# Where the output projection puts its four token tiles between two doubles of the score loop

## The chip, the cores and the metric

The kernel runs on one core of one Trainium2 chip. The metric is the device time of one execution in microseconds (us); of several runs the median is given.

## The reference

Four layers over 2048 tokens of width 448: attention, feed-forward, and both once more with the same weights. All is float32. The attention has 16 query heads of 28 columns and a single head of keys and values.

```
def _A_ref(x, wq, wk, wv, wo):
    q = (x @ wq).reshape(B, S, H, Dh) -> B, H, S, Dh
    k = x @ wk
    v = x @ wv
    scores = jnp.einsum("bhqd,bkd->bhqk", q, k) * (Dh ** -0.5)
    p = _softmax(scores, axis=-1)
    o = jnp.einsum("bhqk,bkd->bhqd", p, v)
    return o -> B, S, H * Dh @ wo

x = A_x
x = x + _A_ref(_layernorm(x, axis=-1), A_wq, A_wk, A_wv, A_wo)
x = x + _B_ref(_layernorm(x, axis=-1), B_w_gate, B_w_up, B_w_down)
x = x + _A_ref(_layernorm(x, axis=-1), A_wq, A_wk, A_wv, A_wo)
x = x + _B_ref(_layernorm(x, axis=-1), B_w_gate, B_w_up, B_w_down)
```

The change concerns the last matmul of the attention, `o @ wo`, and the addition of its result to x.

## The kernel before

**Stages.** For each of the two attention layers the kernel projects queries, keys and values, then runs the score loop (`scores`, line 565), then the feed-forward. Tokens are held in four chunks of 512, each of four token tiles of 128 rows; `xres` holds x in these tiles. The order of instructions on each engine is the order in which the program writes them.

**The score loop.** A group (c, g) is one chunk of 512 queries and four heads; there are 16 groups in a layer. A group has 16 steps, one for each 128 keys (kt). A step n (line 595) issues 12 score matmuls, three passes (z) over four heads (j): the contraction has 32 rows, and the four heads lie in the four 32-row parts of TensorE. Heads 0 to 2 go to the three banks of a triple, `threes[n % 2]`, head 3 goes to a single bank. ACT then takes the exponentials: in an even step the single bank first (L616), then the triple (L617); in an odd step the triple (L611), and, from a copy `raw` that DVE has made of the single bank (L613), head 3 (L614).

Two steps, 2d and 2d + 1, make a double d. After its odd step come `pv(d - 1)` (line 640), the product of the previous double's exponentials with the values, into a single bank that DVE then adds to an accumulator (L657), and `between(d)` (line 620).

**PSUM.** Of eight banks, six are the two triples, and two are single banks:

```
single = lambda d: banks[6 + d % 2]
three, one = threes[n % 2], single(n // 2 + n)   # step n
free, one = threes[0], single(d + 1)                # between(d)
po = single(d + 1)                                  # pv(d)
```

So in double d the even step's head 3 goes to `single(d)`, the odd step's to `single(d + 1)`, and pv(d - 1) to `single(d)`, after the even step's exponential has read it. When `between(d)` runs, the even step's triple `threes[0]`, the odd step's single bank and the bank of pv(d - 1) hold nothing that later work needs, once their readers are done. The next double's even step writes `threes[0]` and `single(d + 1)`, its odd step writes `threes[1]` and `single(d)`.

**The output projection.** When all four groups of a chunk are normalised, the chunk is put on `todo`, and `between` takes it from there at kt equal 10. This happens for chunks 0, 1 and 2, so three times in a layer; chunk 3 is projected after the loop by other lines. `outproj(c, t, po)` (line 582) issues 12 matmuls for one token tile t, four groups by three products of high and low parts, into bank `po`, and returns a function that issues the add of `po` to `xres` on DVE (L591). In the kernel before, tiles 1, 2 and 3 go to the three banks of `threes[0]`; their three adds are issued after all 36 matmuls; then tile 0 goes to the odd step's single bank, with its add behind it.

The function `forward` is called a second time under a condition on the softmax's sums (`full` is true there); that second pass is not run with these inputs.

Of the kernel before, what the change touches and what calls it, by code (L numbers as in the profile page):

```python
# [52 lines left out]
def forward(  # L53
# [278 lines left out]
    class Attention:  # L332
# [232 lines left out]
        def scores(self, ff):  # L565
            next(switch)
            with tc.tile_pool(name=f"at{self.layer}", bufs=1, reuse_waits="tile") as wp:
# [4 lines left out]
                single = lambda d: banks[6 + d % 2]  # L572
# [9 lines left out]
                def outproj(c, t, po, gs=range(NG)):  # L582
                    oh, ol = on[c]
                    ts_ = slice(P * t, P * t + P)
                    for g in gs:
                        for z, (a, b) in enumerate(((oh, woh), (oh, wol), (ol, woh))):
                            nc.tensor.matmul(
                                po[:, 0:D], a[:, g, ts_], b[:, g, :], start=(g + z == 0), stop=(g == NG - 1 and z == 2)
                            )
                    if gs[-1] == NG - 1:  # L590
                        return lambda: nc.vector.tensor_tensor(  # L591
                            xres[:, 4 * c + t, :], po[:, 0:D], xres[:, 4 * c + t, :], ALU.add
                        )
# [26 lines left out]
                def between(d):  # L620

                    i, kt = divmod(2 * d, NT)
                    free, one = threes[0], single(d + 1)
                    if full:
                        self.lent = free[:, 0, :]
                        if 6 <= kt < 14:
                            self.advance(min(NM // 4, NM * (i + 2) - self.done))
                        if kt == 14 and i + 1 < len(GR):
                            self.places[i + 1](free[:, 1, :])
                    if not todo or kt != 10:  # L630
                        return
                    c = todo.pop()
                    adds = []
                    for t in (1, 2, 3):
                        adds.append(outproj(c, t, free[:, t - 1, :]))
                    for f in adds:
                        f()
                    outproj(c, 0, one)()

                def pv(d):  # L640

# [66 lines left out]
                for n in range(last):  # L708
                    i, kt = divmod(n, NT)
                    if kt == 0 and i + 1 < len(GR):  # L710
                        self.parts(i + 1)
                    if kt == 3 and i + 1 < len(GR) and not full:
                        self.rows(i + 1)
                    if kt == 12 and i + 2 < len(GR):
                        self.stack(i + 2)
                    if i in (2, 3) and kt == 8:
                        load_wo(i - 2)
                    if n == NT and ff.nxt:
                        ff.nxt.below(nc.sync)
                    if kt == 8 and 10 < i <= 11 + FG:  # L720
                        ff.W[i - 11] = weights(i - 11)
                    step(n)
                    if not full and n == 1:
                        self.maxima(NC - 1, (6,))
                    if n in later:
                        later.pop(n)()
                    d, odd = divmod(n, 2)
                    if odd:
                        if d:
                            pv(d - 1)  # L730
                        between(d)
                        if d in due:
                            due.pop(d)()
# [322 lines left out]
```

## Time and profile before

| | us |
|---|---|
| median of 3 runs | 1984.74 |
| lowest and highest run | 1983.31, 1984.76 |
| the profiled execution, its time | 1984.76 |
| the profiled execution, its span | 1983.0 |
| exponentials of the score loop, layer 0 | 65.3 to 570.9 |
| exponentials of the score loop, layer 1 | 1047.1 to 1552.5 |
| output projection, L587, inside the loops | 6 times |
| granted TensorE clock | 1.00 |

How to read it: the span runs from the first to the last instruction; the time has a little around it. Engines are PE (TensorE matmul), PEld (its weight loads, which overlap the matmuls), DVE, ACT, POOL and SP. A row of the timeline has the start in us, the length in us, the engine, the line of the kernel, the operation and the tiles as out<-in; in brackets stands how long the engine was idle before it and what ended that. Several like instructions that follow each other are merged, with their count. In names, numbers of buffers are left out: `three` is either triple, `bank` any single bank. A row of the waits has the total, how often, and the longest. The lines themselves stand in the prediction.

### The profile page before, as it was taken

What the parts mean: (1) busy time and instruction counts of PE and PEld (TensorE: products, weight loads), DVE (VectorE), ACT (ScalarE), POOL (GpSimd) and SP (SyncE); (2) the same over time, 40 slices, a digit from 0 to 9 for tenths busy, and PEclk for the clock granted to TensorE, in tenths of its full rate; (3) what the DMA queues carried; (4) which work ended last, traced back from release to release, by engine and by line L of the source; (5) the groups of instructions that cost most, each with busy time, mean ns of one, the idle gap of its engine ahead of it and who ended that gap; (6) DMA issues with size and microseconds to landing.
All of it is one profiled execution on the core that took longest, in us unless ns stands there. A gap on an engine that the chain in (4) does not pass through costs nothing. (4 is left out here: it accounts for less than half of the span.)

```text
span 1983.0 us, 44658 instructions
## 1 busy us (share of the span) xinstructions
PE 1968.8 (99%) x18507; PEld 1323.7 (67%) x18507; DVE 814.1 (41%) x1413; ACT 1277.6 (64%) x2137; POOL 526.5 (27%) x570
## 2 busy tenths in 40 slices
PE   9999999999999999999999999999999999999998
PEld 7544545445458999999984444454454699988887
DVE  7444543544434222322554335435454432222323
ACT  4899797997953333333349998979979533333332
POOL 4212111132213233332341221111222133233320
PEclk9999999999999999999999999999999999999999
DMA  5101020121210011100131111102111100011102
GB/s 163 55 21 31 24 51 22 31 58 28 72 33 6 27 32 32 32 21 22 51 107 35 30 31 30 44 12 59 32 52 48 33 17 25 23 32 32 32 1 76
DMA packets 93382, 77.52 MB, mean 39 GB/s; under 512 B 23510, under 2 KB 76374, under 8 KB 93174
## 3 DMA queue, kind: packets, MB, share of 16 engines
q1 hardware_dynamic: 92886, 74.16, 13.5%
q8 instruction: 146, 2.39, 0.5%
q14 instruction: 62, 0.51, 0.1%
q10 hardware_dynamic: 288, 0.46, 0.1%
HBM read 55.06 MB, written 18.74 MB: 37 GB/s over the span
## 5 line engine op out<-in xcount | busy, mean ns | idle before, releaser
L647 PE MATMUL bank<-pt,vsb 128*32 128x512 f32 x4096 | 493.3, 598 | 0.5
L604 PE MATMUL bank<-qstack,keys 32*128 32x512 f32 x1536 | 484.1, 424 | 1.7 <-DVE xres L591 1.7
L604 PE MATMUL three<-qstack,keys 32*128 32x512 f32 x4608 | 461.4, 425 | 1.5 <-DVE vt L538 1.2
L604 PEld LDWEIGHTS three<-qstack,keys 32*128 32x128 f32 x4608 | 254.1, 182 | 295.3 <-ACT pt L617 181.1
L321 PE MATMUL bank<-xh,wgh 64*128 64x512 f32 x1728 | 437.7, 389 | 0.1
L611 ACT ACTIVATE pt<-three 128x1536 f32<-128x1536 f32 x256 | 372.3, 1454 | 0.6 <-ACT pt L617 0.3
L617 ACT ACTIVATE pt<-three 128x1536 f32<-128x1536 f32 x256 | 372.1, 1453 | 0.0
L321 PE MATMUL bank<-xh,wgl 64*128 64x512 f32 x1404 | 363.1, 390 | 0.0
L321 PE MATMUL bank<-xl,wgh 64*128 64x512 f32 x1296 | 328.5, 389 | 0.0
L321 PE MATMUL bank<-wdh,h 64*128 64x448 f32 x1776 | 327.0, 363 | 0.3 <-ACT h L892 0.2
L891 DVE TENSOR_TENSOR sg<-bank,sg 128x512 f32<-128x512 f32 x111 | 76.7, 691 | 493.4 <-ACT sg L890 484.3
L647 PEld LDWEIGHTS bank<-pt,vsb 128*32 128x32 f32 x4096 | 107.1, 109 | 250.2 <-issue 152.6
L613 DVE COPY raw<-bank 128x512 f32<-128x512 f32 x256 | 177.3, 693 | 230.6 <-PE bank L604 227.7
L321 PEld LDWEIGHTS bank<-xh,wgh 64*128 64x128 f32 x1728 | 256.8, 184 | 16.1 <-issue 0.9
L798 POOL TENSOR_TENSOR xres<-stage,xres 128x448 f32<-128x448 f32 x107 | 126.7, 1206 | 490.2 <-ACT stage L797 490.2
L657 DVE TENSOR_TENSOR o<-bank,o 128x512 f32<-128x512 f32 x224 | 154.8, 691 | 240.9 <-PE bank L647 236.3
L321 PEld LDWEIGHTS bank<-wdh,h 64*128 64x128 f32 x1776 | 238.6, 184 | 12.9 <-issue 2.0
L604 PEld LDWEIGHTS bank<-qstack,keys 32*128 32x128 f32 x1536 | 243.7, 183 | 4.5 <-DVE xres L591 3.6
L328 ACT COPY seen<-bank 128x1 f32<-128x1 f32 x660 | 80.5, 163 | 237.0 <-PE bank L321 234.6
L321 PEld LDWEIGHTS bank<-xh,wgl 64*128 64x128 f32 x1404 | 212.1, 184 | 13.3
L321 PE MATMUL bank<-wdl,h 64*128 64x448 f32 x888 | 213.7, 367 | 0.0
L890 ACT ACTIVATE sg<-bank 128x512 f32<-128x512 f32 x111 | 66.7, 601 | 221.2 <-PE bank L321 212.2
(136 smaller groups left out, 2265.8 us busy)
## 6 DMA issues: line engine op xcount, KB each, us to landing
o<-rd SPq DMA_DIRECT2D x32, 256.0 KB
qraw<-qd SPq DMA_DIRECT2D x128, 56.0 KB
qd<-stage SPq DMA_DIRECT2D x30, 224.0 KB
xt<-xn SPq DMA_DIRECT2D x28, 224.0 KB
wdr<-in_B_w_down_dram SPq DMA_DIRECT2D x28, 224.0 KB
xn<-xt SPq DMA_DIRECT2D x7, 768.0 KB
wr<-in_B_w_gate_dram SPq DMA_DIRECT2D x28, 192.0 KB
wr<-in_B_w_up_dram SPq DMA_DIRECT2D x28, 192.0 KB
```

The source lines that it names most:

```text
L321: nc.tensor.matmul(po, a, b, start=start, stop=stop, skip_group_check=True)
L328: nc.scalar.copy(seen[:, i : i + 1], po[:, 0:1])
L604: nc.tensor.matmul(three[:, j, :] if j < 3 else one, k[js, kp, ks], q[js, part, :], start=(z == 0), stop=(z == 2), tile_position=(32 * j, 0),)
L611: nc.scalar.activation(pt, three, AF.Exp, scale=SCALE)
L613: nc.vector.tensor_copy(raw, one)
L617: nc.scalar.activation(pt, three, AF.Exp, scale=SCALE)
L647: nc.tensor.matmul(po[32 * j : 32 * j + 32, :], vsb[:, n % NT, :], pts[n][j], start=(n == 2 * d), stop=(n > 2 * d), skip_group_check=True,)
L657: nc.vector.tensor_tensor(acc, in_turn(po), acc, ALU.add)
L798: nc.gpsimd.tensor_tensor(r, s, r, ALU.add)
L890: nc.scalar.activation(by_tile(sg), in_turn(pg[0]), AF.Silu)
L891: nc.vector.tensor_tensor(by_tile(sg), in_turn(pg[1]), by_tile(sg), ALU.mult)
```

## The change

In `between`, the four token tiles are put elsewhere and in another order. Tiles 0 and 1 go to the first two banks of `threes[0]`, and their two adds are issued after these 24 matmuls. Then tile 2 goes to the odd step's single bank `single(d + 1)`, with its add behind it. Then tile 3 goes to `single(d)`, the bank of pv(d - 1), which the next double's odd step writes; its add comes last. `outproj` and all else is as before.

```
-                    adds = []
-                    for t in (1, 2, 3):
-                        adds.append(outproj(c, t, free[:, t - 1, :]))
-                    for f in adds:
+                    for f in [outproj(c, t, free[:, t, :]) for t in range(2)]:
                         f()
-                    outproj(c, 0, one)()
+                    outproj(c, 2, one)()
+                    outproj(c, 3, single(d))()
```

## The prediction

> **What bounds the kernel now.** I read the page first, then the waits, then the two attention stages as stretches, then the timeline around one output projection.
>
> ```profile
> span 1983.0 us, 44658 instructions
> PE 1968.8 (99%) x18507; PEld 1323.7 (67%) x18507; DVE 814.1 (41%) x1413; ACT 1277.6 (64%) x2137; POOL 526.5 (27%) x570
> ```
>
> PE looks full, but that is an average over stages, and as matmuls are pipelined and their ends modelled, a busy PE is not PE at its peak. The change touches only the score loop, so that stage decides. The two loops as stretches (span, then busy time and instructions of PE, PEld, DVE, ACT, POOL):
>
> ```profile
> 65.30:575.00 509.70, 507.92 (x5269) 228.97 (x5270) 230.96 (x414) 475.26 (x514) 109.17 (x111) 1.00 0.14 36
> 1048.00:1560.00 512.00, 510.77 (x5284) 231.43 (x5277) 230.76 (x414) 474.87 (x514) 108.41 (x108) 1.00 0.14 35
> ```
>
> ACT is busy for 475.3 of 509.7 us. The rest must be few, large holes, and the waits say which (total, times, longest):
>
> ```profile
> ACT pt L616 <- PE bank L604: 63.6, 8, 10.7
> ...
> PEld bank L604 <- DVE xres L591: 3.6, 6, 0.6
> ```
>
> Nearly all the time that ACT waits for scores lies in 8 places, the longest 10.7 us. Here is one, in ACT's timeline (start, length, idle before it in brackets):
>
> ```profile
> 203.82 1.46 ACT L611 ACTIVATE pt<-three 128x1536 f32<-128x1536 f32 x1
> 205.17 0.62 ACT L614 ACTIVATE pt<-raw 128x512 f32<-128x512 f32 x1
> 216.26 0.60 ACT L616 ACTIVATE pt<-bank 128x512 f32<-128x512 f32 x1 [10.47 <-PE bank L604]
> 216.76 1.45 ACT L617 ACTIVATE pt<-three 128x1536 f32<-128x1536 f32 x1
> 218.09 1.46 ACT L611 ACTIVATE pt<-three 128x1536 f32<-128x1536 f32 x1
> 219.44 0.62 ACT L614 ACTIVATE pt<-raw 128x512 f32<-128x512 f32 x1
> 219.96 0.59 ACT L616 ACTIVATE pt<-bank 128x512 f32<-128x512 f32 x1
> ```
>
> Away from the hole the four exponentials of a double run back to back: from one L616 to the next is 219.96 - 216.26 = 3.70 us, with no idle. So ACT sets the pace of the score loop, and the only time to be had from this change is the hole of 10.47 us, in which PE does the output projection of one chunk. It occurs three times in a layer (line 630: the doubles with kt equal 10 in the group after a finished chunk), six times in all. The last one looks the same as the first, both at the add and at ACT:
>
> ```profile
> 1454.62 0.62 DVE L591 TENSOR_TENSOR xres<-bank,xres 128x448 f32<-128x448 f32 x1 [0.67 <-PE bank L587]
> ```
>
> ```profile
> 1456.34 0.60 ACT L616 ACTIVATE pt<-bank 128x512 f32<-128x512 f32 x1 [10.45 <-PE bank L604]
> ```
>
> **Inside the hole.** The timeline of PE and its neighbours:
>
> ```profile
> 202.81 0.69 DVE L613 COPY raw<-bank 128x512 f32<-128x512 f32 x1 [1.12 <-PE bank L604]
> ...
> 204.50 0.47 PE L587 MATMUL three<-woh,onh 128*128 128x448 f32 x1
> ...
> 204.69 0.69 DVE L657 TENSOR_TENSOR o<-bank,o 128x512 f32<-128x512 f32 x1 [1.19 <-PE bank L647]
> ...
> 209.26 0.37 PE L587 MATMUL three<-woh,onl 128*128 128x448 f32 x1
> 209.47 0.36 PE L587 MATMUL three<-woh,onh 128*128 128x448 f32 x1
> ...
> 211.70 0.36 PE L587 MATMUL three<-woh,onl 128*128 128x448 f32 x1
> 211.90 0.36 PE L587 MATMUL bank<-woh,onh 128*128 128x448 f32 x1
> 212.17 1.69 DVE L591 TENSOR_TENSOR xres<-three,xres 128x448 f32<-128x448 f32 x3 [6.79 <-PE three L587]
> ...
> 214.13 0.36 PE L587 MATMUL bank<-woh,onl 128*128 128x448 f32 x1
> 214.42 0.19 PEld L604 LDWEIGHTS three<-qstack,keys 32*128 32x128 f32 x3 [0.30 <-issue]
> 214.42 0.50 PE L604 MATMUL three<-qstack,keys 32*128 32x512 f32 x3
> 214.53 0.62 DVE L591 TENSOR_TENSOR xres<-bank,xres 128x448 f32<-128x448 f32 x1 [0.67 <-PE bank L587]
> 215.21 0.18 PEld L604 LDWEIGHTS bank<-qstack,keys 32*128 32x128 f32 x1 [0.60 <-DVE xres L591]
> 215.21 0.50 PE L604 MATMUL bank<-qstack,keys 32*128 32x512 f32 x1 [0.28 <-DVE xres L591]
> ...
> 215.21 0.73 PE L604 MATMUL three<-qstack,keys 32*128 32x512 f32 x6
> ...
> 215.56 0.39 PE L604 MATMUL bank<-qstack,keys 32*128 32x512 f32 x1
> 215.78 0.39 PE L604 MATMUL bank<-qstack,keys 32*128 32x512 f32 x1
> ```
>
> The 36 matmuls into the triple run from 204.50 to 211.70, the 12 into the single bank from 211.90 to 214.13, about 0.20 us apart. The next even step starts at 214.42 with its three matmuls into the triple. Its fourth goes to the single bank that the projection has just filled, and that bank is free only when the last add (214.53 to 215.15) has read it: the fourth starts at 215.21, and everything behind it on PE, the six matmuls into triples among it, also at 215.21. ACT's first exponential needs the third matmul into that bank (215.78 + 0.39 = 216.17) and starts at 216.26.
>
> What the step looks like without that wait is seen one double later:
>
> ```profile
> 218.77 0.50 PE L604 MATMUL three<-qstack,keys 32*128 32x512 f32 x3
> 218.78 0.49 PE L604 MATMUL bank<-qstack,keys 32*128 32x512 f32 x1
> ...
> 219.11 0.39 PE L604 MATMUL bank<-qstack,keys 32*128 32x512 f32 x1
> ...
> 219.34 0.39 PE L604 MATMUL bank<-qstack,keys 32*128 32x512 f32 x1
> ```
>
> The fourth starts 0.01 us after the first three, and the later ones into its bank 0.33 and 0.56 us after it. In the hole the fourth came 0.79 us after the first, so 0.78 us of the hole is the wait for the last add.
>
> **The change, part by part.** The same 48 matmuls and 4 adds are issued at each place; no DMA is touched, and POOL has no part in it. Only the targets and the order differ.
>
> 1. Tiles 0 and 1 take 24 matmuls into two banks of the even triple. They start when the first exponential of that triple allows it, as now, at 204.50, and the 24th is at 209.26. Their two adds can follow it instead of the 36th. The triple is free some 4 us before the next even step. Cost nothing, covered by the 24 matmuls behind them; without that cover they would cost what the three adds take, 1.69 us at most.
>
> 2. Tile 2 takes 12 matmuls into the odd step's single bank, in the slots from 209.47 to 211.70. The copy that empties this bank (202.81 to 203.50) is long done. Its add follows the 36th matmul as the first add does now (212.17), takes 0.62 us and ends at 212.79. The next even step wants the bank at 214.43. The 0.78 us wait is gone, hidden behind tile 3's 12 matmuls.
>
> 3. Tile 3 takes 12 matmuls into the other single bank, from 211.90 to 214.13. It must wait for the accumulating add of the previous PV product (L657, 204.69 to 205.38), which is 6.5 us earlier. No wait. Its own add stands where the last add stands now: 214.53 to 215.15, seen by PE at 215.21.
>
> 4. The new wait: the next odd step's fourth matmul now needs that add. Without the old stall the even step goes 214.42, 214.76, 214.99 for its three passes (spacing 0.34 and 0.23 from the undisturbed step), so the odd step starts at about 215.22 and wants the bank at 215.23. The add is seen at 215.21. The wait is between 0 and some 0.1 us if the add slips a little. What queues behind it is the rest of the odd step and then the PV product. PV needs the exponential of the even step's single bank anyway, which ends at 0.60 after ACT's restart, while the odd step's last pass is issued 0.3 us earlier than that; and the odd triple is wanted by ACT only 1.83 us after the restart (218.09 - 216.26). A slip of 0.1 us is therefore hidden. One of over 0.3 us would begin to push PV, and with it the next even step, which has only 0.14 us to spare (219.34 + 0.39 + 0.09 = 219.82 against ACT's 219.96).
>
> A sentence of the Trainium skill bears on part 4: TensorEngine Tiling (Array Packing), Key Properties, says that different tiles load weights and multiply in parallel, independent of each other. Taken as independent issue, it would let the odd step's other three row tiles pass the one that waits, and the new wait could not cost anything; the six triple matmuls held until 215.21 show that a waiting row tile holds the others. The sum is 0.78 us a place by either.
>
> So ACT restarts at 214.43 + 0.56 + 0.39 + 0.09 = 215.47 or 215.48 instead of 216.26, 0.78 us earlier. The trace itself attributes only 0.60 us of idle weight loading to the add, which I take as the lower bound of the gain; the upper is 0.79. I take 0.78, since it compares starts of the same matmuls in two steps, where the 0.60 leaves out that the first loads overlap the wait.
>
> Sum: 6 x 0.78 = 4.7 us (bounds 3.6 and 4.7). As ACT has no other holes from there to the end of the loop, what follows moves up whole; the transfers of the loop are hidden and are issued earlier with it. The profiled execution took 1984.76 us (span 1983.0 and 1.76 around it), which is the median of the runs (1984.74) for this purpose. 1984.76 - 4.7 = **1980.1 us**, 0.24% less.
>
> **Rivals.**
>
> *The release stays where it is.* The next even step's fourth matmul could be let go by the newest add, or tile 2's add could start only after tile 3's matmuls, as the three adds of the triple now all wait for the 36th matmul though the first bank was full after 12. Then the fourth matmul starts at 215.21 again and the time is 1984.7. For it: that late start of the adds, 212.17. Against: in the code the three adds were placed behind all 36 matmuls, whereas tile 2's add is placed ahead of tile 3's matmuls; and the first three matmuls of the step started at 214.42, before the newest add was done, so they waited for their own tile's adds alone. The change then does not do what it says. 8%.
>
> *Half is given back.* The odd step's new wait slips far enough to hold PV. If tile 3's add were seen 0.85 us late, at 216.06, the margins of part 4 (about 0.3 and 0.14 us) leave some 0.4 us for ACT: 6 x 0.4 = 2.4 us of loss against 4.7 of gain, 1982.4. For it: the slack is thin. Against: DVE has nothing to do from the third add to that one. 4%.
>
> *Slower: the projections wait for the adds.* If each single-bank projection waited for the newest DVE instruction ahead of it rather than for the one that emptied its bank, tile 2 would wait for the adds of tiles 0 and 1, and tile 3 for the add of tile 2. The delays are taken from the rows: from a matmul's start to the add 0.47 us (211.70 to 212.17), from the add's end to PE 0.06 (215.15 to 215.21). Tile 2: 209.26 + 0.47 + 1.15 (two adds, 1.69 less one spacing of 0.54) + 0.06 = 210.94 instead of 209.47, 1.47 us. Tile 3: 211.70 + 0.47 + 0.62 + 0.06 = 212.85 instead of 211.90, 0.95 us. Less the 0.78 saved that is 1.64 us a place, 9.8 us, 1994.6. It would turn the gain into a loss from a wait of 0.78 us a place. Against it: now tile 0's first matmul is at 211.90, 0.20 us after its predecessor, though the three adds stand ahead of it in the program and run until 213.86. 4%.
>
> **How the numbers follow.** The forecast has 84%. Its own range is 1978.7 to 1981.2: the three runs of before lie 1.4 us apart, and the lower bound of the gain adds 1.1 us. To reach the case in between, the range is 1978.6 to 1982.4, some 86% with the tails. What a measurement here can tell from no change is about 0.2%, 4.0 us; the gain of 4.7 is only just over it. Within the forecast I give 85% to more than 4.0 us, so faster 0.84 x 0.85, about 0.72; slower 0.04; the rest, 0.24, is within.
>
> **What would show it.** ACT's six holes before L616 fall from 10.47 to about 9.7 us (63.6 us in 8 waits to about 59). The wait of the score matmul into the single bank for the add (3.6 us, 6 times, 0.6 longest) shrinks to under 0.6 us in all, or stands at the odd step. The step's fourth matmul starts within 0.02 us of its first three. The adds stand as two together near 209.7, one near 212.2, one near 214.5. Tile 2's and tile 3's first matmuls come 0.20 us after their predecessors; a gap of some 1 us there is the slower rival, a hole of still 10.4 us with the adds so placed is the first. If the holes shrink and the time does not, ACT was not the bound that I take it for.

## The result and the profile after

The changed kernel takes 1979.7 us (median of 10 runs, 1978.56 to 1980.23); the kernel before, in runs beside it, 1984.3 us. The ratio is 0.9975, with a 95% interval of 0.9966 to 0.9985: faster by a quarter of a per cent, 4.6 us. The forecast was 1980.1 us, 0.24% less.

The page of the changed kernel (the kernel before had a span of 1983.0 us):

```profile
span 1978.3 us, 44658 instructions
PE 1966.2 (99%) x18507; PEld 1326.6 (67%) x18507; DVE 814.5 (41%) x1413; ACT 1278.1 (65%) x2137; POOL 526.4 (27%) x570
```

The instruction counts are the same, and the busy times of DVE, ACT and POOL are within 0.5 us of those before. The gain has to be looked for in waits. Those of the changed kernel (total, times, longest):

```profile
ACT pt L616 <- PE bank L604: 59.0, 8, 9.9
...
DVE xres L591 <- PE three L587: 26.2, 6, 4.4
```

ACT's wait for scores falls from 63.6 to 59.0 us in the same 8 places, which are the six holes and the first exponential of each loop (0.33 us). That is 4.6 us and the whole gain. The row that had the score matmul's weight load wait for the add of the projection (3.6 us, 6 times) is gone from the list.

One of the six places, from the timeline of the changed kernel:

```profile
204.03 0.47 PE L587 MATMUL three<-woh,onh 128*128 128x448 f32 x1
...
209.26 1.16 DVE L591 TENSOR_TENSOR xres<-three,xres 128x448 f32<-128x448 f32 x2 [4.35 <-PE three L587]
...
211.42 0.36 PE L587 MATMUL bank<-woh,onh 128*128 128x448 f32 x1
...
211.62 0.63 DVE L591 TENSOR_TENSOR xres<-bank,xres 128x448 f32<-128x448 f32 x1 [1.20 <-PE bank L587]
...
213.65 0.36 PE L587 MATMUL bank<-woh,onl 128*128 128x448 f32 x1
...
213.94 0.50 PE L604 MATMUL three<-qstack,keys 32*128 32x512 f32 x3
...
213.95 0.49 PE L604 MATMUL bank<-qstack,keys 32*128 32x512 f32 x1
...
214.05 0.62 DVE L591 TENSOR_TENSOR xres<-bank,xres 128x448 f32<-128x448 f32 x1 [1.80 <-PE bank L587]
...
214.52 0.18 PEld L604 LDWEIGHTS three<-qstack,keys 32*128 32x128 f32 x3
214.73 0.18 PEld L604 LDWEIGHTS bank<-qstack,keys 32*128 32x128 f32 x1
...
215.01 0.60 ACT L616 ACTIVATE pt<-bank 128x512 f32<-128x512 f32 x1 [9.69 <-PE bank L604]
...
215.30 0.39 PE L604 MATMUL bank<-qstack,keys 32*128 32x512 f32 x1
...
215.66 1.92 PE L645 MATMUL bank<-pt,vsb 128*32 128x512 f32 x16
...
216.84 1.46 ACT L611 ACTIVATE pt<-three 128x1536 f32<-128x1536 f32 x1
```

Reading down: two adds follow the 24th matmul; tile 3's first matmul is at 211.42, in step with its neighbours 0.20 us apart, so it waited for nothing; tile 2's add runs from 211.62 beside tile 3's matmuls. The even step's fourth matmul starts at 213.95, 0.01 us after its first three, where it came 0.79 us after them before. The last add runs 214.05 to 214.67 beside the even step, and the odd step's weight load for the same bank starts at 214.73, just behind it. ACT's hole is 9.69 us.

That the two loops alone hold the gain is seen at their ends, in ACT's timeline: the first exponential and the table load behind the last.

```profile
64.76 0.60 ACT L616 ACTIVATE pt<-bank 128x512 f32<-128x512 f32 x1 [0.33 <-PE bank L604]
```

```profile
568.18 1.28 ACT L888 ACT_TABLE_LOAD   x1
```

```profile
1044.44 0.60 ACT L616 ACTIVATE pt<-bank 128x512 f32<-128x512 f32 x1 [0.33 <-PE bank L604]
```

```profile
1547.61 1.28 ACT L888 ACT_TABLE_LOAD   x1
```

The loops take 503.4 and 503.2 us; before they took 505.6 and 505.4 (65.3 to 570.9, 1047.1 to 1552.5). That is 2.2 us each, 4.4 in all. The other 0.3 of the 4.7 us between the two spans is what is left of a start that was 0.54 us shorter in this execution and feed-forward stages that were some 0.3 longer; the change has no part in either.

### The profile page after: what moved, and what is told of

It reads as the page before. It is cut to its first block, busy times and chain, and to the rows that moved or that the text cites. A ratio compares the mean times of both kernels' runs of the same rounds, so it can differ in the third digit from the quotient of the medians.

```text
span 1978.3 us, 44658 instructions
## 1 busy us (share of the span) xinstructions
PE 1966.2 (99%) x18507; PEld 1326.6 (67%) x18507; DVE 814.5 (41%) x1413; ACT 1278.1 (65%) x2137; POOL 526.4 (27%) x570
## 5 line engine op out<-in xcount | busy, mean ns | idle before, releaser
L611 ACT ACTIVATE pt<-three 128x1536 f32<-128x1536 f32 x256 | 372.4, 1455 | 0.6 <-ACT pt L617 0.3
L617 ACT ACTIVATE pt<-three 128x1536 f32<-128x1536 f32 x256 | 371.9, 1453 | 0.0
L655 DVE TENSOR_TENSOR o<-bank,o 128x512 f32<-128x512 f32 x224 | 155.0, 692 | 240.6 <-PE bank L645 236.0
```

Of the source, the lines that this page charges most:

```text
L611: nc.scalar.activation(pt, three, AF.Exp, scale=SCALE)
L617: nc.scalar.activation(pt, three, AF.Exp, scale=SCALE)
L655: nc.vector.tensor_tensor(acc, in_turn(po), acc, ALU.add)
```

## The experiments

**One word of the kernel before.**

```
-                    outproj(c, 0, one)()
+                    outproj(c, 0, single(d))()
```

> The kernel before with one word changed: tile 0, still the last of the four, goes to the bank of pv(d - 1), the next odd step's last, instead of to the next even step's. Tiles 1 to 3 stay in the triple with their adds behind 36 matmuls. Theory (the whole gain is the even step's fourth score matmul no longer waiting for the last add): the holes of ACT fall from 10.47 to 9.7 us as in the changed kernel, time 1979.7 us, ratio to the kernel before 0.9975 to 0.998. Rival (the earlier adds of the triple have a part in it, by freeing the triple sooner): the holes stay above 9.9 us and the time lies between 1981 and 1984.

Measured: 1980.29 us, ratio 0.9978 (0.9969 to 0.9988). One of its 11 executions took 9953.9 us; why is not known, and the median does not move by it. The waits of this kernel:

```profile
ACT pt L616 <- PE bank L604: 59.3, 8, 9.9
...
DVE xres L591 <- PE three L587: 41.0, 6, 6.9
```

and, of the kernel before,

```profile
DVE xres L591 <- PE three L587: 40.9, 6, 7.0
```

One hole:

```profile
216.14 0.60 ACT L616 ACTIVATE pt<-bank 128x512 f32<-128x512 f32 x1 [9.71 <-PE bank L604]
```

The adds of the triple are as late here as in the kernel before (DVE waits 41.0 us for them, where it waited 40.9), and the holes are those of the changed kernel. So the bank of the last tile alone brings the gain; that fewer tiles go to the triple, and that its adds come sooner, adds nothing that these runs can tell.

**The two single banks exchanged.**

```
-                    outproj(c, 2, one)()
-                    outproj(c, 3, single(d))()
+                    outproj(c, 2, single(d))()
+                    outproj(c, 3, one)()
```

> The changed kernel with the two single banks exchanged: tile 2 goes to the bank of pv(d - 1), tile 3, the last, to the even step's. Theory: the add of the last tile is again what the even step's fourth score matmul waits for, 0.78 us a place; the holes are 10.47 us again and the time is that of the kernel before, 1984.3 us, ratio 0.9995 to 1.0005. Rival (the triple's early adds or the split into one tile for each bank bring the gain, not the bank of the last): 1980 to 1982 us. Tile 2's bank is wanted 2.4 us sooner after the PV product here; its accumulating add ends 0.9 us after PE is free, and 24 matmuls cover that.

Measured: 1984.87 us, ratio 0.9999 (0.9990 to 1.0008). Its waits:

```profile
ACT pt L616 <- PE bank L604: 63.5, 8, 10.5
...
PEld bank L604 <- DVE xres L591: 3.6, 6, 0.6
```

The wait is back with the very 3.6 us, though the triple's adds are as early as in the changed kernel (DVE waits 26.2 us for them in both). Undoing the bank of the last tile undoes all of the gain.

**The triple last.**

```
+                    outproj(c, 2, one)()
+                    outproj(c, 3, single(d))()
                     for f in [outproj(c, t, free[:, t, :]) for t in range(2)]:
                         f()
-                    outproj(c, 2, one)()
-                    outproj(c, 3, single(d))()
```

> The changed kernel with tiles 2 and 3 (single banks) first and tiles 0 and 1 (the triple's banks) last, their two adds behind all. Theory: now the even step's first score matmul waits for two adds, 0.47 + 1.16 + 0.06 = 1.69 us after the last projection matmul's start where it took 0.29, so 1.40 us are added to a hole of 9.70: 11.1 us, 6 x 1.40 = 8.4 us more than the changed kernel, 1988.1 us, ratio to the kernel before 1.002. Rival (what counts is only the single bank of the fourth matmul, the triple is never what is waited for): 1979.7 us.

Measured: 1988.17 us, ratio 1.0017 (1.0008 to 1.0026). Its waits and one hole:

```profile
ACT pt L616 <- PE bank L604: 68.0, 8, 11.3
...
PEld three L604 <- DVE xres L591: 10.2, 6, 1.7
```

```profile
215.80 0.60 ACT L616 ACTIVATE pt<-bank 128x512 f32<-128x512 f32 x1 [11.09 <-PE bank L604]
```

Now the step's first matmul waits for two adds. The hole of 11.09 us is 1.40 us above the changed kernel's, as worked out from a matmul's start to its add, two adds, and the add's end to PE; 0.54 us of it is the second of the two adds (1.16 us for two, 0.62 for one). With the same 48 matmuls and 4 adds at each place the kernel thus takes 1980, 1984 or 1988 us, by which banks are filled last.

**Two visits.** Two tiles at kt 10, two at kt 12:

```
-                    if not todo or kt != 10:
+                    if not todo or kt not in (10, 12):
                         return
-                    c = todo.pop()
...
+                    c = todo.pop() if kt == 12 else todo[-1]
+                    t = kt - 10
+                    outproj(c, t, free[:, 0, :])()
+                    outproj(c, t + 1, single(d))()
```

> A version that may beat both: the projection of a chunk is made in two visits, two tiles at kt 10 and two at kt 12, each visit one tile to the triple's first bank and then one to the bank of pv(d - 1). No add is waited for in either. It tells who has time to spare in a double. If PE is about as full as ACT (from the trace some 0.12 us of each double's 3.70 are free on PE's matmul row), the two holes together are 9.6 us and the time is 1979 to 1979.7. If PE has the 0.3 + 0.36 us a double that its weight loads show as idle, the second visit hides that much more: two holes of together 9.1 us, 1975.8 to 1977.5.

Measured: 1980.95 us, ratio 0.998 (0.9971 to 0.9989), not below the changed kernel and 1.3 us above the first theory's 1979 to 1979.7. Waits and the first two holes:

```profile
ACT pt L616 <- PE bank L604: 59.6, 14, 5.1
```

```profile
212.31 0.60 ACT L616 ACTIVATE pt<-bank 128x512 f32<-128x512 f32 x1 [4.85 <-PE bank L604]
```

```profile
220.96 0.60 ACT L616 ACTIVATE pt<-bank 128x512 f32<-128x512 f32 x1 [4.85 <-PE bank L604]
```

Twice 4.85 is 9.70, the one hole's length to 0.01 us; five of the six second visits have 4.93 or 4.94 us. A second visit hides nothing, so a double has no time that PE could use for it, and the idle time of the weight loads (0.3 and 0.36 us a double) is not such time. The rows suggest why, though no run tests it. In the changed kernel's trace one PV product starts at 215.66; the add L655 (217.72 to 218.41) empties its bank, which the next odd step's fourth matmul takes at 218.47; that bank's later passes follow at 218.81 and 219.03, and the next PV product at 219.36. From PV to PV that is 3.70 us, as long as ACT's four exponentials. PE waits in this chain, but cannot run ahead in it. What is left of the hole is 48 matmuls of 0.20 us, and the one other placement that was tried does not hide it.

**The last add made late.** An extra DVE copy of tile 3's bank ahead of its add, result unused, of 64 columns, 448 columns, or 448 columns twice:

```
-                    outproj(c, 3, single(d))()
+                    f = outproj(c, 3, single(d))
+                    for n in (448, 448):
+                        nc.vector.tensor_copy(wp.tile([P, D], F32, name="spare")[:, 0:n], single(d)[:, 0:n])
+                    f()
```

> The changed kernel with an extra DVE copy of 64 columns of tile 3's bank ahead of its add (result unused), which makes that add, and so the release of the odd step's bank, later by some 0.15 us. Theory, with the margins of the prediction (0.3 us before PV is pushed, then 0.14 before ACT is): hidden, holes of 9.70 us and no new idle time of ACT. Rival (PV follows the odd step at once, so only the 0.14 us are there): a new ACT wait of under 0.1 us one double later.

> The same with an extra copy of 448 columns, the release later by some 0.55 us. Theory, margins 0.3 + 0.14: holes of 9.70 us as before, and one double later a new ACT wait before L616 of 0.1 us, 0.6 us in all. Rival (only 0.14): a new wait of 0.4 us, 2.4 us in all.

> The same with two extra copies of 448 columns, the release later by some 1.1 us. Theory, margins 0.3 + 0.14: holes of 9.70 us and a new ACT wait of 0.65 us one double later, 3.9 us in all, time 1983.6. Rival (only 0.14): new waits of 0.95 us, 5.7 us in all, 1985.4 us: the gain is lost from a release about 0.9 us late on.

Measured: 1979.62 us (one run), 1981.91 us (one run), and 1986.87 us, ratio 1.0015 (1.0005 to 1.0024). With 64 columns the release is waited for, and ACT's list has no new wait:

```profile
PEld bank L604 <- DVE xres L591: 0.9, 6, 0.2
```

```profile
215.05 0.18 PEld L604 LDWEIGHTS bank<-qstack,keys 32*128 32x128 f32 x1 [0.15 <-DVE xres L591]
...
215.21 0.60 ACT L616 ACTIVATE pt<-bank 128x512 f32<-128x512 f32 x1 [9.88 <-PE bank L604]
...
217.11 1.45 ACT L611 ACTIVATE pt<-three 128x1536 f32<-128x1536 f32 x1
```

With 448 columns, ACT's waits:

```profile
ACT pt L616 <- PE bank L604: 59.2, 8, 9.9
ACT pt L611 <- PE bank L648: 2.6, 8, 0.4
```

and from its timeline:

```profile
214.57 0.61 DVE L591 TENSOR_TENSOR xres<-bank,xres 128x448 f32<-128x448 f32 x1
...
214.99 0.60 ACT L616 ACTIVATE pt<-bank 128x512 f32<-128x512 f32 x1 [9.89 <-PE bank L604]
...
216.13 1.92 PE L648 MATMUL bank<-pt,vsb 128*32 128x512 f32 x16
...
217.31 1.45 ACT L611 ACTIVATE pt<-three 128x1536 f32<-128x1536 f32 x1 [0.38 <-PE bank L648]
```

With two copies, in the timeline:

```profile
214.73 0.60 ACT L616 ACTIVATE pt<-bank 128x512 f32<-128x512 f32 x1 [9.70 <-PE bank L604]
214.97 0.61 DVE L591 TENSOR_TENSOR xres<-bank,xres 128x448 f32<-128x448 f32 x1
...
215.63 0.49 PE L604 MATMUL bank<-qstack,keys 32*128 32x512 f32 x1 [0.77 <-DVE xres L591]
215.64 0.50 PE L604 MATMUL three<-qstack,keys 32*128 32x512 f32 x3
...
216.20 0.39 PE L604 MATMUL bank<-qstack,keys 32*128 32x512 f32 x1
216.52 1.92 PE L648 MATMUL bank<-pt,vsb 128*32 128x512 f32 x16
...
217.70 1.45 ACT L611 ACTIVATE pt<-three 128x1536 f32<-128x1536 f32 x1 [1.02 <-PE bank L648]
```

The holes are those of the changed kernel in all three (9.70 us in most places, about 9.88 in some, as there), but behind them something is lost. How much has to be read from start to start. Rows of ACT overlap: in the changed kernel L617 runs to 215.51 + 1.44 = 216.95, and L611 starts at 216.84. A start that is late by up to 0.11 us therefore shows no idle time, and a longer delay shows 0.11 us too little of it. Measured from ACT's restart (L616) in the first of the six places, in us:

| last add | release of the bank | first PV matmul | L611 | next double's L616 |
|---|---|---|---|---|
| changed kernel | -0.28 | 0.65 | 1.83 | 3.70 |
| one copy, 64 columns | -0.16 | 0.73 | 1.90 | 3.77 |
| one copy, 448 columns | 0.25 | 1.14 | 2.32 | 4.18 |
| two copies, 448 columns | 0.90 | 1.79 | 2.97 | 4.83 |

The release comes later by 0.12, 0.53 and 1.18 us, and the next double by 0.07, 0.48 and 1.13, in all six places to within 0.02. So the margin is about 0.05 us, well below the rival's 0.14 and far from the 0.44 of the prediction; not even the copy of 64 columns is hidden, against its theory (its rival's under 0.1 us is the right size, at another place), though 6 x 0.07 us is too little to be seen in the time of one run. With two copies 6 x 1.13 = 6.8 us are lost; the medians, of different sets of runs, lie 7.2 us apart. The place is another one too: not first L616 a double later, but the odd step's own exponential of the triple, L611, which waits for PV. It follows PV's first matmul by 1.17 or 1.18 us in all four rows of the table, so it has nothing to spare behind PV.

**What the late PV stops.** L611 writes one of three buffers, the one that PV's first half has to have read. Room for a fourth was made by leaving out the low part of the attention output in the projection (its product is replaced by a repeat of the second); the pair of runs differs in the number of buffers only.

```
-                    pt = wp.tile([P, 3, 512], F32, name="pt", bufs=3)
+                    pt = wp.tile([P, 3, 512], F32, name="pt", bufs=4)
```

> Control for the next run: the kernel with two extra copies, which also leaves out the low part of the normalised attention output (its product is replaced by a repeat of the second, so the matmuls stay 12 a tile and the sum is slightly off; one POOL instruction a group falls away). That makes room in SBUF. Both theories: as with two extra copies alone, six new ACT waits of about 1.0 us before L611, on PV.

> The control with four buffers for the exponentials of a triple instead of three. What is in question is through what the late PV product stops ACT: the odd step's exponential L611 writes the buffer that PV's first half reads, and the next even step of scores follows PV on PE. Theory A (both are about equally tight): the waits before L611 vanish and come back one instruction pair later, before L616 of the next double, at about 1.0 us each, 5 to 6 us in all, with the time unchanged. Theory B (the buffer alone is tight): the waits vanish, L616 keeps its six holes of 9.7 to 9.9 us and gains under 0.2 us a place, the time falls by some 5 us.

Measured: 1986.58 and 1985.17 us, one run each. ACT's waits with three buffers,

```profile
ACT pt L616 <- PE bank L604: 59.6, 8, 9.9
ACT pt L611 <- PE bank L648: 6.6, 8, 1.0
```

and with four, with the row that follows the first hole:

```profile
ACT pt L616 <- PE bank L604: 66.6, 16, 10.0
```

```profile
218.95 0.60 ACT L616 ACTIVATE pt<-bank 128x512 f32<-128x512 f32 x1 [1.22 <-PE bank L604]
```

With four buffers the waits on L611 are gone, and 7.0 us more are waited before L616 in eight further places: theory A. A late PV stops ACT by the buffer first, and by the next even step's scores if the buffer is taken out of the way. From start to start the next double's L616 is then late by 1.03 us in four of the six places, where L611 was late by 1.14 with three buffers, so the even step has some 0.11 us to spare behind PV; in the other two it is late by 1.31, and why is not shown. The time is 1.4 us lower than the control's, one run against one, where theory A had it unchanged.

## Why the prediction was right, point by point

*What bounds the loop.* It held that the time to be had from this change lies in ACT's six holes: the one shown fell by 0.78 us (10.47 to 9.69), all together by 4.6, and the span by 4.7. "ACT sets the pace" may be half of it: in the two visits a double had no time left on PE either, and the rows show the chain of PV, add and odd step to be as long as ACT's double.

*Tiles 0 and 1, cost nothing.* Right: the two adds start 5.23 us after the first projection matmul and end long before the next step. The price without the cover, at most 1.69 us, was right in size: with the triple last two adds cost 1.40 us net.

*Tile 2, the 0.78 us wait is gone.* Right, and shown to be the cause from both sides: the bank of the last tile alone brings it, and the exchange of the banks takes it back.

*Tile 3, no wait.* Right: its first matmul follows its predecessor by 0.20 us.

*The new wait of the odd step, 0 to 0.1 us, hidden.* It was there: the odd step's weight load for that bank starts at 214.73, 0.06 us behind the add, while those for its triple start at 214.52. On PE its first two passes into the bank are 0.32 us apart (214.75 and 215.07) where 0.23 is usual, so it costs PE 0.09 us. It was hidden, as forecast: L611 starts 1.83 us after ACT's restart, as before the change. But only about 0.05 us was left in hand.

*The margin of that cover was mis-sized.* The prediction has PV pushed only by a slip of over 0.3 us, and then the next even step with 0.14 us to spare. The first was wrong, because it counted from the issue of the odd step's last pass to the end of ACT's exponential and left out the time from that pass to the first PV matmul: 0.32 us in the run with two copies (216.20 to 216.52), where the last two passes of the step are 0.23 apart. In the changed kernel the two are 0.36 us apart (215.30 to 215.66), so PV has 0.04 us to spare, not 0.3. The second is near what four buffers show, 0.11, but it is not what stops ACT first: with three buffers L611 waits for PV's first half, a wait that the prediction does not have, and nothing is to spare there. The rival "half is given back" was thereby priced too low: by the measured margin, 0.85 us late would have cost about 0.8 us a place, 4.8 us, all of the gain. It did not come about because the release was on time.

*The other rivals.* The release did not stay with the newest add (fourth matmul at 213.95, that add until 214.67), and the projections did not wait for the adds ahead of them (0.20 us at both seams).

*The Trainium skill's sentence.* TensorEngine Tiling (Array Packing), Key Properties, has tiles load and multiply in parallel, independent of each other. The trace agrees for matmuls that wait for nothing: the first three of the even step start together at 213.94, the fourth 0.01 us later. It shows no independent issue: in the run with two copies the odd step's triple matmuls of the second pass stand at 215.64, behind the one that waited for the add until 215.63. So a row tile that waits holds those behind it. In the kernel before it held three triple matmuls until 215.21, and not six as the prediction has it: the row of six there lasts 0.73 us and spans two passes, the later of which follows at about the usual spacing.

## What to carry to other kernels

Where one engine fills several banks in a burst and another must empty them, the bank filled last should be the one that the next work asks for last; the order costs nothing and was worth 0.78 to 1.40 us a burst here. The price is read from one row, the first matmul that starts late behind its siblings, and it counts fully only while the engine that it starves has no slack. Before trusting a cover, measure it up to the next engine's start, with the changes of matmul shape and every buffer that this engine needs: a cover that looked 0.44 us deep was 0.05. And measure a delay from start to start: where rows of an engine overlap, as ACT's do by 0.11 us here, the idle time shows too little.

## What the runs showed of the hardware

From the last 32-row score matmul to the first PV matmul of 32 columns PE took 0.32 us in the run with two copies, where the profile shows no other engine that PV waited for. From the last full matmul of the projection to the first 32-row one it took 0.29 (213.65 to 213.94 in the changed kernel). Matmuls of the projection follow each other in 0.20 us and passes of the score steps in 0.23, but the second pass behind such a change, or behind a wait, in 0.34 (215.63 to 215.97 with two copies). No run sets the change of shape apart from what else happens at these places. The prediction left the first of these times out of its cover.
